# Attention, convolution-gated FFN and spatially gated FFN on one core: a new order of all engines' work

## The chip, the cores and the metric

The kernel runs on one core of a Trainium2 chip. A core has TensorE (PE: matrix multiplications, with its weight loads shown apart as PEld), VectorE (DVE), ScalarE (ACT), GpSimd (POOL) and SyncE (SP), which here only issues DMAs. The metric is the device time of one launch in microseconds (us); lower is better.

## The reference

Three stages follow each other, all in fp32; the output of each is the input `x` of the next.

```python
# attention: q, k, v are (4, 8, 576, 64); block = 64
scores = scale * q @ k.T;  scores = where(block_i >= block_j, scores, -1e9)
attn = exp(scores - max(scores));  attn = attn / (sum(attn) + 1e-9);  out = attn @ v
# first FFN: x is (4, 576, 512), w_in (512, 1024), conv_w (3, 1024), w_out (1024, 512)
h = max(x @ w_in, 0);  conv_out[s] = sum over k of conv_w[k] * h[s + k - 1]
x = (h * sigmoid(conv_out)) @ w_out
# second FFN: w_in (512, 1024), w_spatial (576, 576), w_out (512, 512)
h = max(x @ w_in, 0);  u, v = h[..., :512], h[..., 512:]
v_n = (v - mean(v)) / sqrt(var(v) + 1e-6)
v_s = einsum('ts,bsd->btd', w_spatial, v_n) + b_spatial[:, None]
out = (u * v_s) @ w_out
```

## The kernel before

**Precision.** TensorE reads a 4-byte type with fewer mantissa bits (fp32r) at one pass a column. Each operand is therefore split in a high part, `hi = round(x)`, and a low part, `lo = x - hi`, and a product is three matmuls (hi·hi, lo·hi, hi·lo). In the names of the trace `kp`, `qp` are the high parts of a pair's keys and queries, and the low parts are written over the loaded data in `raw`; `x` holds the two parts of what goes into the first FFN, `w1i_h`, `w1i_l`, `w1o_h`, `w1o_l` those of its weights. A split is two operations (a cast or rounding, then a subtraction), and each can stand on any of ACT, DVE and POOL.

**Steps.** PE's program is a row of 432 steps. The letters of the string `SEQ` say of which kind the next one is:

- `x`: of a pair of heads (there are 16 pairs) four steps that give block scores for a bound on each row's maximum (L943, and L661 for the last block, whose queries stand in `qlast`), and a fifth that transposes the collected maxima `mx` (L1005). DVE reduces the four into `mx` (L948, L983, L986), joins them (L996, task `max_up`), and after the transpose `mt` goes by DMA into a row `mq` (L1018). So x20 to x23 are pair 4's maxima and x24 its transpose.
- `s`: four steps a pair with the masked scores (L1062 in plain fp32 in some pairs, L1070 with split operands in the others; L1074 adds the row `mq`), each followed by an exponential on ACT (L1083). The score buffers `st` are three, shared with the maxima and `v`.
- `v`: attention times values (L669). ACT or DVE then copies the sums into `srow` (L1173) and the product into `xp` (L1164), which frees the buffer. The sums go by two DMAs through a reciprocal (L1188) and come back as `rb`; `xp` times `rb` (L1202) is split into `x`.
- `m`: first FFN (L661): up to 12 matmuls of 288 or 290 columns each. Those that end the FFN are taken out of `mo` by ACT or DVE as `y` (L1276, L1277).
- `p`: second FFN, at the end; `f`: filler.

`x`'s block steps, `s` and `v` use PE's array split in parts of 64 rows or columns (the trace shows 64\*128 or 128\*64), transposes, `m`, `p` and the last block's step the whole array (128\*128). I call these split mode and whole mode.

**Order.** Nothing is left to the hardware or to a compiler's scheduler. `SEQ` fixes PE's order; the tables `ORDER` fix the order of tasks on DVE, ACT, POOL and of DMAs on SP's queue, `ENG` gives for each operation that can be done by several engines the one that does it, and `BIND` which buffer of a ring each step takes. Every engine takes its list strictly in order: an operation that waits holds up what stands behind it. The constants of a planner (`od.cost += ...`) stand beside the matmuls; with all tables given they no longer choose an order.

**Data.** The keys and queries of a pair come in one 576 KB load (L868) into `raw`; there are three such buffers, and in a pair with split operands the loaded data leave theirs when both low parts have been written to another one; pair 5's load waits in this way for pair 3's low parts. Weights of the first FFN come as `w_raw` and `x` halves (L810) and are put together by a copy `top` (L817) and DVE (L820), task `split64`.

Of the kernel before, what the change touches and what calls it, by code (L numbers as in the profile page):

```python
# [1873 lines left out]
```

## Time and profile before

| | us |
|---|---|
| three runs | 578.92, 580.26, 580.30; median 580.26 |
| profiled execution | 579.51 |
| its span, from the first to the last instruction | 577.7 |
| PE busy | 567.5 (98% of the span) |
| DVE, ACT, POOL busy | 420.0, 260.1, 121.3 |

The time of the profiled execution is 1.8 us more than its span; that share lies outside the instructions. A row of the timeline gives start, length, engine, line, operation, output and inputs, sizes, the count of equal operations joined in it, and in brackets the idle time of the engine just before it with what ended that. Matmuls overlap, so for PE the distance from one start to the next is the step of its clock, not the length of one. The granted clock of TensorE is 1.00 over the whole span.

### The profile page before, as it was taken

The page shows a single profiled execution, that of the slowest core. Times are in us where ns is not written, and L with a number is a line of the kernel's source. Part 1 is how long each engine was busy: PE and PEld are TensorE (multiplying, and loading weights), DVE is VectorE, ACT ScalarE, POOL GpSimd, SP SyncE. Part 2 cuts the span into 40 slices and gives each one's busy share as a digit, 9 for nine tenths or more (in the row PEclk, how much of TensorE's full clock was granted, in tenths as well). Part 3 has the DMA queues.
Part 4 walks back from the last instruction along what each step waited for, and adds up shares of the span by engine and source line. Part 5 has one row for each costly group of instructions (what it writes and reads, how often), then busy time and mean ns, then how long its engine had stood idle before and what let it go on. Part 6 is the DMA issues. An engine that isn't in the chain of part 4 may idle for free.

```text
span 577.7 us, 11721 instructions
## 1 busy us (share of the span) xinstructions
PE 567.5 (98%) x4570; PEld 510.3 (88%) x4570; DVE 420.0 (73%) x954; ACT 260.1 (45%) x554; POOL 121.3 (21%) x166
## 2 busy tenths in 40 slices
PE   7999999999999999999999999999999999999997
PEld 5667689798988888899989999999999989999997
DVE  5779889978498889859575788566996445456557
ACT  5657668643566336447353766443351014004101
POOL 3334312130012222400311020333111111012020
PEclk9999999999999999999999999999999999999999
DMA  6666652031404134040214547137303230340002
GB/s 214 222 198 210 211 176 64 31 117 44 125 24 138 55 127 127 15 135 2 65 43 147 194 143 215 43 114 249 101 1 124 71 92 1 124 116 8 32 32 83
DMA packets 43430, 61.13 MB, mean 106 GB/s; under 512 B 8877, under 2 KB 34221, under 8 KB 43374
## 3 DMA queue, kind: packets, MB, share of 16 engines
q1 hardware_dynamic: 43226, 60.37, 32.8%
q8 instruction: 36, 0.59, 0.4%
q14 instruction: 20, 0.16, 0.1%
q10 hardware_dynamic: 148, 0.01, 0.0%
HBM read 45.99 MB, written 14.23 MB: 104 GB/s over the span
## 4 chain that ended last, share of the span: by engine, by line
PE 92%; DMA 2%; ACT 2%; DVE 2%; POOL 1%; issue 1%; SPq 0%; ACTq 0%; DVEq 0%; POOLq 0%
PE mo L661 55%; PE s L661 14%; PE st L669 10%; PE st L1070 4%; PE st L1062 3%; PE st L943 2%; PE st L1074 2%; PE st L661 1%; DMA raw<-in_kq_dram 1%; DMA cwr<-in_cw_dram 1%; ACT e L1083 1%; DVE y L1668 0%; POOL x L698 0%; PE st L1005 0%; ACT top L817 0%
## 5 line engine op out<-in xcount | busy, mean ns | idle before, releaser
L661 PE MATMUL mo<-x,w1i_h 128*128 128x290 f32 x504 | 105.6, 299 | 0.4 <-DVE y L1277 0.4
L661 PE MATMUL mo<-g,w1o_h 128*128 128x288 f32 x464 | 97.7, 297 | 0.0
L661 PEld LDWEIGHTS mo<-x,w1i_h 128*128 128x128 f32 x504 | 82.4, 189 | 2.2 <-DVE y L1277 0.6
L661 PEld LDWEIGHTS mo<-g,w1o_h 128*128 128x128 f32 x464 | 76.0, 189 | 2.0 <-issue 1.6
L1240 DVE SCALAR_TENSOR_TENSOR cc<-h,cwt,cc 128x288 f32<-128x288 f32 x128 | 66.4, 532 | 12.5 <-ACT cc L1237 11.5
L661 PE MATMUL mo<-x,w1i_l 128*128 128x290 f32 x252 | 74.8, 297 | 0.0
L661 PE MATMUL mo<-g,w1o_l 128*128 128x288 f32 x232 | 68.5, 295 | 0.0
L1083 ACT ACTIVATE e<-st 128x1024 f32<-128x1024 f32 (+2 forms) x64 | 53.2, 838 | 21.3 <-PE st L1074 20.4
L661 PE MATMUL mo<-x,w2i_h 128*128 128x288 f32 x256 | 51.8, 295 | 0.0
L948 DVE TENSOR_REDUCE mx<-st 128x2 f32<-128x128 f32 (+2 forms) x64 | 42.5, 684 | 9.6 <-PE st L943 9.2
L661 PEld LDWEIGHTS mo<-x,w1i_l 128*128 128x128 f32 x252 | 47.5, 189 | 0.0
L669 PE MATMUL st<-e,v 128*64 128x448 f32 (+4 forms) x384 | 46.7, 392 | 0.1
L669 PEld LDWEIGHTS st<-e,v 128*64 128x64 f32 x384 | 25.0, 137 | 22.9 <-issue 17.0
L661 PEld LDWEIGHTS mo<-g,w1o_l 128*128 128x128 f32 x232 | 43.6, 188 | 0.0
L672 POOL TENSOR_SCALAR g<-ga 128x288 fp32r<-128x288 f32 x40 | 20.2, 516 | 110.5 <-DVE ga L1588 44.1
L661 PEld LDWEIGHTS mo<-x,w2i_h 128*128 128x128 f32 x256 | 41.2, 188 | 0.4 <-ACT u L1562 0.3
L698 POOL TENSOR_TENSOR g<-cc,g 128x288 fp32r<-128x288 f32 x19 | 18.1, 953 | 105.8 <-ACT g L691 70.3
L661 PE MATMUL s<-w2i_h,x 128*128 128x512 f32 x128 | 39.5, 390 | 0.0
L661 PE MATMUL mo<-ws_h,vnh 128*128 128x288 f32 x135 | 39.4, 296 | 0.0
L661 PE MATMUL mo<-x,w2i_l 128*128 128x288 f32 x128 | 37.7, 295 | 0.0
L1074 PE MATMUL st<-mq,mk 64*128 64x320 f32 (+1 forms) x192 | 36.8, 381 | 0.0
L1237 ACT ACTIVATE cc<-h,cwt 128x288 f32<-128x288 f32 x64 | 33.9, 532 | 5.6 <-DVE g L675 2.8
(200 smaller groups left out, 1327.4 us busy)
## 6 DMA issues: line engine op xcount, KB each, us to landing
x2d<-y SPq DMA_DIRECT2D x32, 288.0 KB
x<-x2d SPq DMA_DIRECT2D x16, 576.0 KB
raw<-in_kq_dram SPq DMA_DIRECT2D x15, 576.0 KB
v<-in_vt_dram SPq DMA_DIRECT2D x16, 320.0 KB
rb<-rd SPq DMA_DIRECT2D x32, 144.0 KB
x<-in_w2i_dram SPq DMA_DIRECT2D x8, 512.0 KB
out_dram<-o SPq DMA_DIRECT2D x28, 144.0 KB
w_raw<-in_w1i_dram SPq DMA_DIRECT2D x4, 512.0 KB
```

What stands on the lines that cost most here:

```text
L661: nc.tensor.matmul(o, w, x, start=start, stop=stop)
L669: nc.tensor.matmul(o[row:row + m], w, x, start=start, stop=stop)
L672: nc.gpsimd.tensor_scalar(o, i, 1.0, 0.0, ALU.mult, ALU.add)
L698: P=("POOL", t_ptt(n), lambda: nc.gpsimd.tensor_tensor(o, a, b, ALU.subtract), 0, prio, True))
L943: nc.tensor.matmul(st[:, e, o:o + n], qp[r, 128 * c:128 * c + 128], kp[r, 0:n], start=True, stop=True)
L948: return ("DVE", t_dve(2 * i.shape[-1] * (i.shape[2] if len(i.shape) == 4 else 1)), lambda: nc.vector.tensor_reduce(o, i, AX.X, ALU.max), ...
L1062: nc.tensor.matmul(out, keys(RAW[p][:, 0, :], r), RAW[p][r, 1, q0:q0 + nq], start=True, stop=False)
L1070: nc.tensor.matmul(st[:, e, o:o + nq], keys(kx, slice(64 * e, 64 * e + 64)), qx[e], start=j == 0, stop=False)
L1074: nc.tensor.matmul(st[:, e, o:o + nq], keys(mk, r), q[r, q0:q0 + nq], start=False, stop=True)
L1083: yield ("ACT", t_act(2 * n), lambda: nc.scalar.activation(ex[:, :, e0:e0 + n], st[:, :, 0:n], ACTF.Exp, scale=0.125), 0, 0)
L1237: yield ("ACT", t_act(HT, False, 1), lambda: nc.scalar.activation(cc, h[:, o:o + HT], ACTF.Copy, scale=cwt[:, c, 1:2]), 0, P_G)
L1240: yield ("DVE", t_dve(HT, ptr=1), lambda: nc.vector.scalar_tensor_tensor(cc, h[:, o + e:o + e + HT], cwt[:, c, j:j + 1], cc, ALU.mult, ALU ...
```

## The change

The diff replaces `SEQ`, the tables `ORDER` of DVE, ACT, POOL and SP, most of `ENG`, and a few rows of `BIND`; and constants of the planner. No line that issues an instruction is changed; all lines behind L62 move by one or two numbers. Both programs have the same 432 steps and the same matmuls on PE. ACT's program has 528 operations for 552, POOL's 189 for 161, DVE's 936 for 940.

```diff
 SEQ = (
-    "xxxyxyxsssfsxxssfxyxxvxssssxyxxvxssssxyxxvxssssxyxxvxssssxyxxvsxsfxssyxxvxsmmmmmxxmmxxxmmmmsssmmssvxmxxxmmssxm"
-    "mmmxMmmmxmmmxxvxsmmmxsssssmmmmmmmxmxxvxssmmmmmxvssssssmmmmxxvxssxmmmmxxmxxvssmmxssmxmxmmxxvsxmsssxmxmxxvsmmxsm"
...
+    "xxxyxyxsssfsxxssfxyxxvxssssxyxxvxssssxyxxvxssssxyxxvxssssxyxxvsxsfxyssmxxvxsmmmmmxxmmxxxmmsssssmmmvxxmxxxmmssm"
+    "mmmxMmxmmmxxvmsxmmmmmxmsssssmmmmxmmxxvxssmmmmvxmssssssmmmmmxxvxssxmmmxxmxxvmssxmssmmmxxmxxvxsmsssxmmmxmxxvsxms"
...
-    "KL": "PDPPPDPPDDDDDDPD",
-    "QL": "PDDDPPPDDDDDPDPD",
+    "KL": "PDPPPPPPDDDDDPDD",
+    "QL": "PDDPPDPDDDDDDDPD",
...
-    "X": "PPDDDPDDPDPPDPPD",
+    "X": "PDDDDDPPPDPDDPPD",
...
-    "TOP": "AAAAAAAAAAAAAAAAAAAAAAAA",
+    "TOP": "AAPPPDAPDPDADAAAPDPAPAAA",
...
-        self.cost = (0.12 if self.tile else 0.2) if tile != self.tile else 0.0
+        self.cost = 0.1 if tile != self.tile else 0.0
...
-            od.cost += max(n / 2400 + 0.0145, 0.107)
+            od.cost += max(n / 2400 + 0.0135, 0.107)
...
+            od.cost += 0.18
```

(`KL`, `QL`: subtraction for the low parts of keys and queries, one letter a pair; `X`: that of `x`; `TOP`: the copy `top`; A, D, P are ACT, DVE, POOL.)

**Behind pair 3's scores, POOL.** `raw<-raw,kp` and `raw<-raw,qp` are the low parts of pair 3's keys and queries, `x_624` or `x_625` is the `x` of pair 0 and `x_768` that of pair 1. Before:

```order
L672 TENSOR_SCALAR qlast_153<-raw 64x64
L698 TENSOR_TENSOR raw<-raw,kp_157 128x576
L698 TENSOR_TENSOR x_624<-xp_132,x_624 128x576
L672 TENSOR_SCALAR qlast_153<-raw 64x64
L672 TENSOR_SCALAR kp_155<-raw 128x576
L698 TENSOR_TENSOR w1i_l<-w_f_140,w1i_h 128x4x128
L698 TENSOR_TENSOR x_768<-xp_133,x_768 128x576
```

And after:

```order
L820 CAST top_144<-x_504 128x512
L673 TENSOR_SCALAR qlast_153<-raw 64x64
L699 TENSOR_TENSOR raw<-raw,kp_157 128x576
L699 TENSOR_TENSOR raw<-raw,qp_158 128x576
L699 TENSOR_TENSOR x_625<-xp_132,x_625 128x576
L673 TENSOR_SCALAR w1o_h<-w_f_139 128x512
L820 CAST top_144<-x_649 128x512
L673 TENSOR_SCALAR qlast_154<-raw 64x64
L673 TENSOR_SCALAR kp_157<-raw 128x576
```

POOL now does both low parts of pair 3, no longer the subtraction of pair 1's `x`, and two copies `top` among them.

**The same stretch, DVE,** from pair 4's last maximum (L948 or L949) to its join (L996 or L997) and some rows behind it. Before:

```order
L986 TENSOR_REDUCE mx<-mxl 128x1
L675 TENSOR_TENSOR w1i_l<-w_f_139,w1i_h 128x4x128
L948 TENSOR_REDUCE mx<-st_113 128x2
L948 TENSOR_REDUCE mxu<-st_113 128x2
L692 CAST qp_156<-raw 128x576
L996 SCALAR_TENSOR_TENSOR mx<-mxu,lim,mx 128x8
L1188 RECIPROCAL rc<-rc 36x32
L1202 TENSOR_TENSOR xp_133<-xp_133,rb 128x160
```

And after:

```order
L949 TENSOR_REDUCE mxu<-st_113 128x2
L693 CAST qp_156<-raw 128x576
L1190 RECIPROCAL rc<-rc 36x32
L693 CAST qlast_153<-raw 64x64
L997 SCALAR_TENSOR_TENSOR mx<-mxu,lim,mx 128x8
L1204 TENSOR_TENSOR xp_133<-xp_133,rb 128x160
```

The join stands behind the reciprocal and behind a cast of pair 5's last queries. Further on, ahead of pair 5's join, DVE has these rows after, of which the first, third and sixth have no counterpart on DVE before:

```order
L693 CAST x_775<-xp_133 128x576
L949 TENSOR_REDUCE mx<-st_112 128x2
L676 TENSOR_TENSOR x_775<-xp_133,x_775 128x576
L984 TENSOR_REDUCE mxl<-mo_110 128x1
L949 TENSOR_REDUCE mxu<-st_112 128x2x2
L693 CAST qp_158<-raw 128x576
L676 TENSOR_TENSOR w1o_l<-w_f_139,w1o_h 128x512
L987 TENSOR_REDUCE mx<-mxl 128x1
```

They are the two operations of pair 1's `x`, and a cast of pair 6's queries.

**Around pair 6's transpose, PE.** Before:

```order
L661 MATMUL mo_111<-full 128x222 x2
L1005 MATMUL st_113<-ident,mx 9x128
L1070 MATMUL st_112<-qp_156,kp_155 128x448 x2
L1070 MATMUL st_112<-qp_156,raw 128x448 x2
L1070 MATMUL st_112<-raw,kp_155 128x448 x2
```

And after:

```order
L662 MATMUL mo_111<-full 128x222 x2
L1006 MATMUL st_113<-ident,mx 9x128
L662 MATMUL mo_111<-kp_157,qlast_154 128x288
L662 MATMUL mo_110<-kp_157,qlast_154 128x288
L1071 MATMUL st_112<-qp_156,kp_155 128x448 x2
```

The step that follows the transpose is now one of whole mode.

**Ahead of the step m33, DVE,** where the sums `y` of the first FFN leave `mo`. Before:

```order
L1202 TENSOR_TENSOR xp_133<-xp_133,rb 128x576
L692 CAST x_1911<-xp_133 128x576
L675 TENSOR_TENSOR x_1911<-xp_133,x_1911 128x576
L692 CAST qlast_153<-raw 64x64
L1277 SCALAR_TENSOR_TENSOR y_137<-mo_110,y_137 128x288
```

And after:

```order
L1204 TENSOR_TENSOR xp_133<-xp_133,rb 128x576
L693 CAST x_1898<-xp_133 128x576
L1279 SCALAR_TENSOR_TENSOR y_137<-mo_110,y_137 128x288
L1156 TENSOR_TENSOR es_131<-e_128,e_130 128x896
L1279 SCALAR_TENSOR_TENSOR y_138<-mo_111,y_138 128x288
```

The cast of `qlast` (pair 11) is gone from DVE there, and on PE the step m31, whose sums the first of these `y` takes, stands ahead of the five score steps s35 to s39 and no longer behind them (second row of `SEQ`).

## Rows read from the trace of the kernel before

**Rows 1.** The page: busy time, share of the span, instructions of each engine.

```profile
PE 567.5 (98%) x4570; PEld 510.3 (88%) x4570; DVE 420.0 (73%) x954; ACT 260.1 (45%) x554; POOL 121.3 (21%) x166
```

**Rows 2.** Waits of PE: line, releaser, us in total, times, longest.

```profile
PE st L1005 <- DMA ident<-in_cst_dram: 2.5, 1, 2.5
...
PE st L943 <- ACT e L1083: 0.9, 3, 0.4
PE st L1070 <- ACT e L1083: 0.6, 1, 0.6
PE mo L661 <- DVE y L1277: 0.4, 1, 0.4
PE st L1062 <- ACT xp L1164: 0.4, 1, 0.4
```

**Rows 3.** Timeline of PE, into split mode and back to whole mode.

```profile
95.52 0.29 PE L661 MATMUL mo<-x,w1i_l 128*128 128x290 f32 x1
95.65 0.29 PE L661 MATMUL mo<-x,w1i_h 128*128 128x290 f32 x1
95.87 0.70 PE L1062 MATMUL st<-raw 64*128 64x256 f32 x4
...
99.01 0.40 PE L661 MATMUL mo<-x,w1i_h 128*128 128x290 f32 x1
99.25 0.29 PE L661 MATMUL mo<-x,w1i_l 128*128 128x290 f32 x1
```

**Rows 4.** Timeline of PE at two transposes.

```profile
39.09 0.28 PE L1005 MATMUL st<-ident,mx 128*9 128x128 f32 x1
39.12 0.51 PE L661 MATMUL mo<-kp,qlast 128*128 128x288 f32 x2
...
144.33 0.27 PE L1005 MATMUL st<-ident,mx 128*9 128x128 f32 x1
144.53 0.38 PE L1070 MATMUL st<-qp,kp 64*128 64x256 f32 x2
```

**Rows 5.** Timeline of SP's queue at the start.

```profile
3.69 0.50 SPq L1429 DMA_DIRECT2D ident<-in_cst_dram  x1
```

**Rows 6.** Timelines of POOL, DVE and SP: pair 3's low parts, pair 5's load.

```profile
39.24 1.42 POOL L698 TENSOR_TENSOR raw<-raw,kp 128x576 fp32r<-128x576 f32 x1 [3.65 <-PE st L1074]
...
40.34 0.93 DVE L675 TENSOR_TENSOR raw<-raw,qp 128x576 fp32r<-128x576 f32 x1
...
41.34 0.33 SPq L868 DMA_DIRECT2D raw<-in_kq_dram  x1
```

**Rows 7.** Timelines of DVE and PE up to pair 4's transpose.

```profile
46.98 0.46 DVE L692 CAST qp<-raw 128x576 fp32r<-128x576 f32 x1 [0.42 <-DMA raw<-in_kq_dram]
47.36 0.83 DVE L996 SCALAR_TENSOR_TENSOR mx<-mxu,lim,mx 128x8 f32<-128x8 f32 x1
48.11 0.34 DVE L1188 RECIPROCAL rc<-rc 36x32 f32<-36x32 f32 x1
...
49.03 0.28 PE L1005 MATMUL st<-ident,mx 128*9 128x128 f32 x1
```

**Rows 8.** Timelines of POOL, DVE and ACT from 54 us on.

```profile
54.03 1.87 POOL L698 TENSOR_TENSOR x<-xp,x 128x576 fp32r<-128x576 f32 x1
...
54.54 1.40 DVE L692 CAST qlast<-raw 64x64 fp32r<-64x64 f32 x1
...
55.93 0.65 ACT L1164 ACTIVATE xp<-st 128x576 f32<-128x576 f32 x1 [0.29 <-POOL x L698]
```

**Rows 9.** Timelines of DVE and PE up to pair 5's transpose.

```profile
57.90 0.21 DVE L996 SCALAR_TENSOR_TENSOR mx<-mxu,lim,mx 128x8 f32<-128x8 f32 x1
...
59.82 0.28 PE L1005 MATMUL st<-ident,mx 128*9 128x128 f32 x1
```

**Rows 10.** Timeline of DVE ahead of m33.

```profile
151.37 0.76 DVE L675 TENSOR_TENSOR x<-xp,x 128x576 fp32r<-128x576 f32 x1
153.58 0.18 DVE L692 CAST qlast<-raw 64x64 fp32r<-64x64 f32 x1 [1.45 <-DMA raw<-in_kq_dram]
```

More of the change, by code (lines that the diff above doesn't have):

```diff
@@ L64 @@
 SEQ = (
-    "xxxyxyxsssfsxxssfxyxxvxssssxyxxvxssssxyxxvxssssxyxxvxssssxyxxvsxsfxssyxxvxsmmmmmxxmmxxxmmmmsssmmssvxmxxxmmssxm"
-    "mmmxMmmmxmmmxxvxsmmmxsssssmmmmmmmxmxxvxssmmmmmxvssssssmmmmxxvxssxmmmmxxmxxvssmmxssmxmxmmxxvsxmsssxmxmxxvsmmxsm"
-    "mssmmmxmmmmmmmmmMmmmmmmsvsssmmmmmvmmmmmmmmmmmmmmmmmmmmMmmmmmmmmmmmppmmmmMmmmpppppppppppppppppppppppppppppppppp"
+    "xxxyxyxsssfsxxssfxyxxvxssssxyxxvxssssxyxxvxssssxyxxvxssssxyxxvsxsfxyssmxxvxsmmmmmxxmmxxxmmsssssmmmvxxmxxxmmssm"
+    "mmmxMmxmmmxxvmsxmmmmmxmsssssmmmmxmmxxvxssmmmmvxmssssssmmmmmxxvxssxmmmxxmxxvmssxmssmmmxxmxxvxsmsssxmmmxmxxvsxms"
+    "mssmmmmmmmmmxmmmMmmmmmmssvmssmmmmvmmmmmmmmmmmmmmmmmmmmMmmmmmmmmmmmppmmmmMmpmmppppppppppppppppppppppppppppppppp"
     "pPppPpPpPPpPppppppPpppppppppppppppppppPPPPPPppPPPppppPppppppppppppppppppPPPPPPppPppppppppPpppPpPpPpPpp"
@@ L241 @@
     ),
+    "mq": (
+        "x4:0 x9:1 x14:2 x19:0 x24:1 x29:2 x34:0 x39:1 x44:2 x49:0 x54:1 x59:2 x64:0 x69:1 x74:2 x79:0"
+    ),
+    "e0": (
+        "s0:0 s6:1 s10:0 s14:1 s18:0 s22:1 s26:0 s30:1 s34:0 s38:1 s42:0 s46:1 s50:0 s54:1 s58:0 s62:1"
+    ),
     "wf": (
         "split64:0 split64.2:1 split64.3:0 split64.4:1 split64.5:0 split64.6:1 split64.7:0 split64.8:1 split64.9:0 "
[3 rows of a table removed]
[3 rows of a table added]
     ),
@@ L251 @@
         "split643.2:0 split643.3:0 split643.4:0 split643.5:0 split643.6:0 split643.7:0 split643.8:0"
-    ),
-    "e0": (
-        "s0:0 s6:1 s10:0 s14:1 s18:0 s22:1 s26:0 s30:1 s34:0 s38:1 s42:0 s46:1 s50:0 s54:1 s58:0 s62:1"
-    ),
-    "mq": (
-        "x4:0 x9:1 x14:2 x19:0 x24:1 x29:2 x34:0 x39:1 x44:2 x49:0 x54:1 x59:2 x64:0 x69:1 x74:2 x79:0"
     ),
@@ L276 @@
     ),
-    "es": (
-        "add_up6:0 add_up7:0 add_up8:0 add_up9:0 add_up10:0 add_up11:0 add_up12:0 add_up13:0 add_up14:0 add_up15:0"
-    ),
     "g": (
@@ L284 @@
         "m104:0 m105:1 m106:2 m107:3 m116:4 m117:5 m118:6 m119:7 m120:8 parts0B110POOL:9 parts0B111POOL:a "
[6 rows of a table removed]
[6 rows of a table added]
         "parts3B210POOL:7 parts3B211POOL:a p120:0 p121:1 parts3T20ACT:3 parts3T30ACT:8 parts3B220POOL:9 parts3T21ACT:2 "
[1 row of a table removed]
[1 row of a table added]
+    ),
+    "es": (
+        "add_up6:0 add_up7:0 add_up8:0 add_up9:0 add_up10:0 add_up11:0 add_up12:0 add_up13:0 add_up14:0 add_up15:0"
     ),
@@ L300 @@
     "cc": (
[4 rows of a table removed]
[4 rows of a table added]
     ),
     "y": (
-        "m14:0 m15:1 m18:0 m19:1 m27:0 m28:1 m31:0 m32:1 m46:0 m47:1 m51:0 m50:1 m59:1 m60:0 m63:0 m64:1 m78:1 m79:0 "
-        "m83:1 m82:0 m91:1 m92:0 m95:1 m96:0 m110:1 m111:0 m114:1 m115:0 m123:0 m124:1 m127:0 m128:1 prep_p2:01"
+        "m14:0 m15:1 m18:0 m19:1 m27:0 m28:1 m31:0 m32:1 m46:0 m47:1 m50:1 m51:0 m59:1 m60:0 m63:0 m64:1 m78:1 m79:0 "
+        "m82:0 m83:1 m91:1 m92:0 m95:1 m96:0 m110:1 m111:0 m114:1 m115:0 m123:0 m124:1 m127:0 m128:1 prep_p2:01"
     ),
@@ L316 @@
     "vf": (
-        "p0:0 p1:1 p2:0 p3:1 p4:0 p21:1 p22:0 p23:1 p24:0 p59:1 p60:0 p61:0 p62:1 p63:0 p94:1 p95:0 p97:1 p96:0"
+        "p0:0 p1:1 p2:0 p3:1 p4:0 p21:1 p22:0 p23:1 p24:0 p59:1 p60:0 p61:0 p63:0 p62:1 p94:1 p95:0 p97:1 p96:0"
     ),
@@ L328 @@
     "o": (
-        "p33.2:0 p34.2:1 p33.2:2 p33.2:3 p34.2:1 p33.2:0 p34.2:2 p34.2:3 p53.2:1 p54.2:2 p53.2:3 p53.2:0 p54.2:1 "
+        "p33.2:0 p34.2:1 p33.2:2 p33.2:3 p33.2:0 p34.2:1 p34.2:2 p34.2:3 p53.2:1 p54.2:2 p53.2:3 p53.2:0 p54.2:1 "
         "p54.2:2 p53.2:3 p54.2:3 p88.2:0 p89.2:2 p88.2:3 p88.2:1 p89.2:0 p88.2:2 p89.2:3 p89.2:1 p124.2:1 p125.2:0 "
@@ L335 @@
 ENG = {
-    "WH": "APDDPDAAPDPPDAAAADAPPDPD",
-    "W": "PDPPPDDPDDDPDPDDPPPDDPDD",
-    "K": "AAPPDPAAADDADAADP",
-    "Q": "DADAPDAAAAPAAPPDA",
-    "QE": "PPPAAADDPDPADPPAADAADPDAPDDPAPAA",
-    "KL": "PDPPPDPPDDDDDDPD",
-    "QL": "PDDDPPPDDDDDPDPD",
-    "M": "AADDDADDAADAAAAD",
-    "ADD": "PPPPPPPPDDDDPPPPDDDDDDDDDDDDDDPDDDDDDDPDDDDDDDPPDDDDDDDPDDDPDDDD",
-    "V": "AAAADAADAAADADAA",
-    "S": "AAAAAAAAAAADDADA",
-    "XH": "AAAPAADDDPAPPDAD",
-    "X": "PPDDDPDDPDPPDPPD",
-    "GH": "ADAAPAAPPAAADADPDAAAADDPPDPAAAAADAADPDADPDDPDAADDAADAADAAADAAPPA",
-    "G": "DPPDDPDDDPPDDPDDDPPPPDDPDDDDDPPDDPDDDDDPPPDDDDDPDDDDDDDDDDDPDDDD",
-    "TOP": "AAAAAAAAAAAAAAAAAAAAAAAA",
+    "WH": "PAPPAAPDPPDPPADPDAPPADDA",
+    "W": "PPDPDPDDDDDDDPDDDPPDDPPP",
+    "K": "AAPDDAPPPAPPDAAAD",
+    "Q": "DPPPDDDAPADPDPADA",
+    "QE": "PAAADAPDPDADPDPADPAPAPAADPDDDDAP",
+    "KL": "PDPPPPPPDDDDDPDD",
+    "QL": "PDDPPDPDDDDDDDPD",
+    "M": "DADDADDAAAAADDAD",
+    "ADD": "PPPPPPPPDDDDPPPPDDDDDDDDDDDPDDDPDPPPDPDDDDDDDDPDDDDPPDDPPDPDDDDD",
+    "V": "AAAAADAAADADDAAA",
+    "S": "AAAAADAAAADDDAAA",
+    "XH": "ADAAAPPDAAAAPDDD",
+    "X": "PDDDDDPPPDPDDPPD",
+    "GH": "AADAAADDDPPAAAPDPPDAAADDPPPPAPAPAAAPADDADPAAAPDDADPAAAAADPAAAAPP",
+    "G": "DDPPPPDDPDPDPPDPDPPDPDPPDPPPDPDDDDDDPPPDDDDDDDDDDDDDDDDDDPDPDPDD",
+    "TOP": "AAPPPDAPDPDADAAAPDPAPAAA",
 }
@@ L667, in tiled @@
             m, n = w.shape[-1], x.shape[-1]
-            od.cost += max(4 * n / 2400, 0.2) / 2 if m == 64 else n / 2400 + 0.022
+            od.cost += max(4 * n / 2400, 0.2) / 2 if m == 64 else n / 2400 + 0.014
             nc.tensor.matmul(o[row:row + m], w, x, start=start, stop=stop)
@@ L816, in split64 @@
         yield alt("TOP", unit,
-                  A=on("A", 512, lambda: nc.scalar.activation(o, x, ACTF.Copy), prio),
+                  A=("ACT", t_act(512, False) + 0.17, lambda: nc.scalar.activation(o, x, ACTF.Copy), 0, prio, False),
                   D=on("D", 512, lambda: nc.vector.tensor_copy(o, x), prio, fast=True),
@@ L943, in fn @@
                     nc.tensor.matmul(st[:, e, o:o + n], qp[r, 128 * c:128 * c + 128], kp[r, 0:n], start=True, stop=True)
-                od.cost += max(n / 2400 + 0.015, 0.105)
+                od.cost += max(n / 2400 + 0.06, 0.16) + (0.055 if i else 0.0)
             def task():
@@ L1005, in fn @@
             nc.tensor.transpose(st[0:NBLK, 0, 0:128], mx[:, 0:NBLK], ident)
-            od.cost += 0.1
+            od.cost += 0.04
             def task():
@@ L1075, in unit @@
             if part is None:
-                od.cost += 5 * nq / 2400 + 0.12 if f32_scores(p) else 4 * max(nq / 2400 + 0.015, 0.105)
+                od.cost += (5 * nq / 2400 + (0.04 if nq > 192 else 0.075) if f32_scores(p) else 4 * max(nq / 2400 + 0.033, 0.076))
             else:
```

239 rows, old and new, of tables (BIND, ORDER) are left out of this document.

## The prediction

> **What bounds the kernel now.** I read the page first: PE is busy for 567.5 of 577.7 us, the next engine, DVE, for 420.0 [rows 1]. The kernel is bound by PE's own row of steps, and since the change keeps every matmul, it can only touch three things: the idle time of PE, the time that PE loses between steps of different kinds, and what the other engines newly make PE wait for. So the second view is the list of what PE waited for [rows 2]. It names one large wait, 2.5 us for the DMA of `ident` ahead of the first transpose, and then a handful of 0.2 to 0.6 us each, of which I copy the largest four kinds, 2.3 us together. Most of these are round trips: PE gives scores, ACT takes the exponential, PE may go on in the freed buffer. The order of PE's steps in that stretch (the first 67 steps, to about 68 us) and the buffers they take are the same after the change, so the three waits of L943 and the one of L1070 for an exponential, 1.5 us, stay. What is there to be won is small, then: the first wait, and two of 0.4 us that are not round trips. What can be lost is not bounded so closely, because between 25 and 100 us DVE is nearly full and runs just ahead of PE.
>
> **Head.** `ident` is the third DMA behind pair 1's load on SP's queue, issued at 3.69 us [rows 5]; after the change it is the first, ahead of a 512 KB weight load. The transpose can then start earlier, by the whole 2.5 us at most. But PE's next steps need more than the transpose: the row `mq` that goes by DMA, ACT's share of the copies around it, and pair 1's 576 KB, which stand behind the same bytes on the queue as before (a 64 KB load that changes places with larger ones ahead of it moves nothing behind it). I take 0.3 us as gained, nearer to the end at which the wait is only moved to the next load; the ends are 0 and −1.6 (the wait falls to the size of one weight load less).
>
> **Pair 3's low parts and pair 5's load.** Before, POOL made the low part of the keys (39.24, 1.42 us) while DVE made that of the queries (40.34, 0.93 us, to 41.27), and SP issued pair 5's load at 41.34, as soon as both were done [rows 6]. After, POOL makes both, one behind the other: 39.24 + 2 × 1.42 = 42.08, so the load starts 0.81 us later. DVE's cast of pair 5's queries at 46.98 waited 0.42 us for that very load [rows 7], so it moves to 47.79 and ends at 48.25. Before, pair 4's join L996 followed at once, and PE's transpose at 49.03 came 0.84 us after the join's end at 48.19. After, the reciprocal (0.34) and a cast of the last queries stand ahead of the join. With an undisturbed cast of 0.18 [rows 10] and join of 0.21 [rows 9] the join ends at 48.25 + 0.34 + 0.18 + 0.21 = 48.98, just in time for 49.03. But while POOL runs, the same two operations took 1.40 and 0.83 [rows 7, 8], and POOL casts pair 5's keys at the same landing; with these the join ends at 50.82, and PE waits 1.8 us. I take 0.4, nearer to the undisturbed end, because only the join's row of this very place is lengthened (by 0.6); ends 0 and 1.8.
>
> A rule of the Trainium skill speaks against this part: "SBUF — State Buffer", section "Who interferes with whom", says that DVE and GpSimd share one pair of ports, held by one of them exclusively, and that the loser is blocked. The rows above agree (1.40 against 0.18 us beside POOL's subtraction of 1.87), and by the rule alone the end at 1.8 would be the one to take; 28 more operations on POOL give it more places.
>
> **Pair 1's `x`.** ACT's copy `xp` at 55.93 stood 0.29 us idle for POOL's subtraction, which ran from 54.03 to 55.90 [rows 8], and PE's L1062 waited 0.4 us for that copy [rows 2]. After, DVE does the cast and the subtraction, in its list well ahead of that point. I count −0.3; the ends are −0.4 and 0 (DVE late too). The price is on DVE: between the joins of pairs 4 and 5 its list has grown by three operations, a cast (0.46, as [rows 7] shows for one of the same size), a subtraction (0.76 [rows 10]) and a cast of pair 6's queries (0.46), 1.68 us together. Pair 5's join ended at 58.11, and the transpose that needs it started at 59.82, 1.71 us later [rows 9]. So the cover is used up to the last 0.03 us. I cost it at nothing, with the next term for what is late beside it.
>
> **The step m33.** On DVE, the sums `y` that free `mo` for m33 stood behind a cast of pair 11's `qlast`, and DVE sat idle 1.45 us until the load had landed [rows 10]; PE lost 0.4 us [rows 2]. After, that cast is gone from DVE, and PE does m31 ahead of s35 to s39, so the sums are ready some microseconds sooner. Ahead of them on DVE stands only the product with `rb`, which needs a DMA of its own; hence 0 as the upper end. I take −0.4, the lower end is −0.55.
>
> **Changes of mode on PE.** The step from 95.65 to 95.87, whole to split mode, took 0.22 against the usual 0.13 (95.52 to 95.65), 0.09 more; on the way back the first matmul took 0.24 (99.01 to 99.25), 0.11 more [rows 3]. Counting along `SEQ`, there are 55 changes before and 63 after, so four pairs more, 4 × 0.20 = 0.80 us. Against it stand three transposes that were followed at once by a step in split mode (pairs 6, 10 and 11): it took 0.20 us to that step (144.33 to 144.53) where a transpose before whole mode takes 0.03 (39.09 to 39.12) [rows 4]. After, all 16 are followed by whole mode, so these three changes cost 0.09 at a later step in place of 0.17: 0.80 − 3 × 0.08 = +0.56. Each price is from one place, and the 0.11 of the way back weighs most; if it is nothing behind the shorter matmuls that end many score steps, 0.44 of this go. I take +0.3, the middle; the ends are 0 and +0.8.
>
> The Trainium skill, "TensorEngine Tiling (Array Packing)", section "Key Properties", says that a change of mode requires the array to drain. Here the rows agree, in the 0.09 and 0.11 above. By the rule alone all eight changes cost, 0.8 us and nothing comes back at the transposes; the sum would be 0.5 higher.
>
> **New waits.** From 70 us to 180 us nearly every step of DVE, ACT and POOL has another place. Where slack was large it is mostly still large, but a wait like that of m33 came up once in 577 us in the order before; I allow +0.3 for one such, ends 0 and +1.2 (a blocked cast as in [rows 8], on the path). The second FFN's steps and the stores at the end stand as they did.
>
> **The sum:** −0.3 + 0.4 − 0.3 − 0.4 + 0.3 + 0.3 = 0.0 us. The profiled execution took 579.51; it lies between the fastest run (578.92) and the median (580.26), 0.75 below the latter. I make the sum against it and forecast 579.5 us, no change. About 1.7 us, 0.3%, is what a measurement can tell from none.
>
> **Rivals.**
>
> *Faster.* The first transpose's wait goes and what it gained is kept to the end: −1.6, with −0.4 for pair 1's `x`, −0.55 for m33, and the other terms at their lower ends, 0: −2.55, 577.0 us. For it speaks that 2.5 us is by far the largest wait, and that PE behind it is limited by nothing but itself for most of the span; against it that pair 1's load and the exponentials' round trips behind it are not moved, and that pair 5's load must not be late. It decides whether pair 4's transpose comes earlier than 49.03.
>
> *Slower.* DVE falls behind pair 5's load. It waits in order for that load ahead of pair 4's join (1.8 us at PE, if POOL disturbs), then carries 1.7 us more work towards pair 5's join with no slack left, of which I count 0.8, and the first steps of the first FFN meet the same late DVE. With the head's 0.3 lost too, and the changes of mode at 0.3 and one new wait at 0.3, less 0.7 for the two waits that go: +1.8 + 0.8 + 0.3 + 0.3 − 0.7 = +2.5, 582.0 us. It decides from the point at which the join of pair 4 ends later than its transpose could start, that is from a delay of the load by more than 0.86 us or one blocked cast. For it speak the two lengthened rows and the thin slack; against it that DVE had idle time of 0.42 at this load and 0.88 a few microseconds on, and that POOL could begin the low parts sooner, having less ahead of it there.
>
> *Nothing moves.* The waits that go come back elsewhere, because most of PE's idle time is round trips of fixed length. That gives 579.5 as well, and I count it with the forecast.
>
> **How the numbers follow.** No change: 0.56. Faster by over 0.3%: 0.21, the first rival with the part of its range that reaches beyond 1.7 us. Slower by over 0.3%: 0.23, the second rival. The range runs from 577.4 to 581.9: below it lies about a third of the first rival's chance, above it somewhat over half of the second's, 2 in 10 together.
>
> **What would show it.** In the profile of the changed kernel: PE's wait for `ident` well below 2.5 us, but pair 4's transpose still within 0.5 us of 49.0; SP's issue of pair 5's load at about 42.2 and DVE's cast behind it ending near 48.3; no wait of PE's L1062 for `xp` beyond 0.2 and none of L661 for `y`; and PE's busy time within 0.5 us of 567.5. I would be wrong if PE's transposes of pairs 4 to 6 wait for `mx` by over 1 us, if the first FFN's steps show waits for `x`, `g` or `y` that together exceed 1 us, or if pair 4's transpose starts before 48.

## The result and the profile after

The changed kernel takes 583.62 us (median of four runs, 582.98 to 583.77), the kernel before on the same chip 579.59: a ratio of 1.0072, 95% interval 1.0055 to 1.0088. On a second chip it was 581.70 against 578.87, 1.0043 (1.0027 to 1.0058). It is slower, by 0.4 to 0.7%, where no change was forecast; the range ended at 581.9. The profiled execution took 583.57, with a span of 581.8 us against 577.7.

The page's first part, in the columns of [rows 1], then PE's waits in those of [rows 2]:

```profile
PE 567.5 (98%) x4570; PEld 510.3 (88%) x4570; DVE 425.5 (73%) x950; ACT 245.7 (42%) x530; POOL 143.1 (25%) x194
```

```profile
PE st L1006 <- DVE mx L997: 3.0, 1, 3.0
PE st L944 <- DVE mxu L949: 1.3, 1, 1.3
...
PE mo L662 <- DVE y L1279: 1.0, 1, 1.0
PE st L1063 <- DVE mxu L949: 1.0, 1, 1.0
PE st L944 <- DVE mt L1012: 0.9, 1, 0.9
PE st L1071 <- ACT e L1084: 0.6, 1, 0.6
PE st L944 <- ACT e L1084: 0.5, 2, 0.3
```

PE is busy for exactly as long as before. All of the loss is idle time, and four waits of about 1 us each that [rows 2] does not have stand for it; all four name DVE. The wait for `ident` is gone from the list, but the first transpose waits no less: the name in front is now the join L997, which was nearly as late before.

Since both programs have the same steps, the starts of the same steps can be set side by side (read from PE's timelines of both kernels):

| step | before | after | later by |
|---|---|---|---|
| first transpose (x4) | 10.26 | 9.88 | −0.38 |
| pair 0, second half of the scores (s4) | 15.84 | 15.64 | −0.20 |
| next score step (s5) | 17.14 | 18.09 | 0.95 |
| pair 2, fourth block step (x13) | 24.37 | 26.73 | 2.36 |
| pair 4, second block step (x21) | 39.56 | 42.08 | 2.52 |
| pair 4, third block step (x22) | 39.90 | 43.52 | 3.62 |
| pair 4's transpose (x24) | 49.03 | 52.63 | 3.60 |
| pair 4's second score step, behind `xp` (s19) | 56.64 | 59.80 | 3.16 |
| pair 6's transpose (x34) | 68.57 | 72.05 | 3.48 |
| m28 | 141.16 | 144.34 | 3.18 |
| m33 | 154.18 | 156.81 | 2.63 |
| m116 | 348.34 | 351.13 | 2.79 |
| m117 | 349.95 | 353.93 | 3.98 |
| last step of the program | 573.21 | 577.14 | 3.93 |

The loss comes in four jumps, at s5 (1.15), x13 (1.41 up to it), x22 (1.10) and m117 (1.19), 4.85 together. Between them 0.7 us net is won, at s19 (0.44) and m33 (0.55) above all. Three of the jumps lie ahead of 45 us, in the stretch in which PE's own order is unchanged.

What DVE did there, in its timeline after:

```profile
16.60 1.24 DVE L781 TENSOR_SCALAR cwr<-cwr 128x24 uint32<-128x24 uint32 x1
17.76 0.28 DVE L949 TENSOR_REDUCE mxu<-st 128x2 f32<-128x128 f32 x1
...
23.88 2.59 DVE L676 TENSOR_TENSOR w1i_l<-w_f,w1i_h 128x512 fp32r<-128x512 f32 x1 [0.86 <-POOL w1i_h L673]
26.40 0.61 DVE L949 TENSOR_REDUCE mxu<-st 128x2 f32<-128x128 f32 x2
...
41.71 1.57 DVE L1204 TENSOR_TENSOR xp<-xp,rb 128x160 f32<-128x160 f32 x1 [0.77 <-DMA rb<-rd]
43.20 0.27 DVE L1012 CAST mt<-st 9x128 fp32r<-9x128 f32 x1
```

And POOL's at the same times:

```profile
16.55 1.26 POOL L699 TENSOR_TENSOR w1i_l<-w_f,w1i_h 128x512 fp32r<-128x512 f32 x1
...
23.81 0.24 POOL L673 TENSOR_SCALAR qlast<-raw 64x64 fp32r<-64x64 f32 x1
24.01 1.28 POOL L699 TENSOR_TENSOR w1i_l<-w_f,w1i_h 128x512 fp32r<-128x512 f32 x1
25.27 0.67 POOL L673 TENSOR_SCALAR qp<-raw 128x576 fp32r<-128x576 f32 x1
...
41.69 1.41 POOL L699 TENSOR_TENSOR raw<-raw,kp 128x576 fp32r<-128x576 f32 x1 [0.63 <-PE st L1075]
```

PE's timeline shows who stood behind each of them:

```profile
18.09 0.54 PE L1063 MATMUL st<-raw 64*128 64x320 f32 x2 [1.02 <-DVE mxu L949]
...
26.73 0.50 PE L944 MATMUL st<-kp,qp 64*128 64x512 f32 x2 [1.32 <-DVE mxu L949]
...
43.52 0.44 PE L944 MATMUL st<-kp,qp 64*128 64x384 f32 x2 [0.94 <-DVE mt L1012]
...
353.93 0.40 PE L662 MATMUL mo<-x,w1i_h 128*128 128x290 f32 x1 [1.03 <-DVE y L1279]
```

Three times the pattern is the same. An operation that PE does not need soon (a bit operation on the convolution weights, the low part of a weight, a product of pair 1) stands in DVE's list ahead of one that PE needs at once (a reduction, the copy `mt`), and POOL works at that moment. The first takes 1.24 us for 24 elements a partition, the second 2.59 us; the same subtraction takes 0.68 where POOL is quiet (below). POOL was first each time, ahead of the second by 0.07 us with a short cast (23.81). At m117 it is another matter: ACT takes m115's sums only at 352.98, and one of the two buffers `y` was still being stored, by a DMA that stood behind a 512 KB load on SP's queue:

```profile
345.78 0.33 SPq L811 DMA_DIRECT2D x<-in_w2i_dram  x1
347.01 0.38 SPq L1282 DMA_DIRECT2D x2d<-y  x1
```

### The profile page after: what moved, and what is told of

It reads as the page before. It is cut to its first block, busy times and chain, and to the rows that moved or that the text cites. A ratio compares the mean times of both kernels' runs of the same rounds, so it can differ in the third digit from the quotient of the medians.

```text
span 581.8 us, 11708 instructions
## 1 busy us (share of the span) xinstructions
PE 567.5 (98%) x4570; PEld 510.3 (88%) x4570; DVE 425.5 (73%) x950; ACT 245.7 (42%) x530; POOL 143.1 (25%) x194
## 4 chain that ended last, share of the span: by engine, by line
PE 94%; DVE 2%; ACT 1%; DMA 1%; issue 1%; SPq 0%; POOL 0%; ACTq 0%; DVEq 0%
PE mo L662 56%; PE s L662 14%; PE st L670 10%; PE st L1071 4%; PE st L1063 3%; PE st L944 2%; PE st L1075 2%; PE st L662 1%; DMA raw<-in_kq_dram 1%; ACT e L1084 1%; DVE w1i_l L676 0%; PE st L1006 0%; DVE mx L949 0%; DVE w_f L821 0%; SPq L860 0%
## 5 line engine op out<-in xcount | busy, mean ns | idle before, releaser
L949 DVE TENSOR_REDUCE mx<-st 128x2 f32<-128x640 f32 (+2 forms) x64 | 42.6, 683 | 5.9 <-PE st L944 5.5
L1246 DVE SCALAR_TENSOR_TENSOR cc<-cc,h 128x288 f32<-128x288 f32 x64 | 29.2, 466 | 10.2 <-ACT cc L1244 10.0
```

The source lines that it names most:

```text
L949: return ("DVE", t_dve(2 * i.shape[-1] * (i.shape[2] if len(i.shape) == 4 else 1)), lambda: nc.vector.tensor_reduce(o, i, AX.X, ALU.max), ...
L1246: yield ("DVE", t_dve(HT), lambda: nc.vector.scalar_tensor_tensor(cc, cc, 1.0, h[:, o:o + HT], ALU.add, ALU.mult), 0, P_G, True)
```

## The experiments

**Theory.** Each of the four jumps is one operation in the wrong place of a list, and the length of DVE's operations there is POOL's doing: moved, each gives its time back. **Rivals.** PE is held by round trips there anyway and the wait comes back (the prediction's "nothing moves"); only DVE's order counts, POOL has no part in it.

**One move at a time.** The first moves the bit operation (task `start2`) behind pair 1's join:

```diff
-x7 ends2 x5 start2 x7 x8*2 max_up1 start2 split64.3
+x7 ends2 x5 x7 x8*2 max_up1 start2*2 split64.3
```

> After the change, with one DVE task moved: the bit operation on the convolution weights (L781, 1.24 us at 16.60, beside a subtraction on POOL from 16.55 to 17.81) stands behind pair 1's join instead of ahead of its last reductions. PE's fourth score step of pair 0 waited 1.02 us for a reduction behind it. Theory 'DVE's list': the time that a DVE operation takes beside POOL, and what is queued behind it, holds PE; then this wait falls below 0.2 us, pair 1's transpose starts near 18.7 instead of 19.61, and the time falls by 0.9 to 1.1 us. Rival 'round trips': PE is held there by the exponentials on ACT in any case, the wait comes back at the next steps, and the shift of all later work stays within 0.3 us of what it was. Rival 'clock': the loss is the granted clock of 0.50 between 9 and 15 us, and the place of this operation changes nothing.

580.97 us against 578.77 of the kernel before on that chip, 1.0039 (1.0021 to 1.0058). The bit operation takes 0.17 us (at 18.07), the wait at s5 is gone, and pair 1's transpose starts at 18.20, by 1.4 us sooner than in the changed kernel. The jump at x13 went with it, without being touched:

```profile
18.07 0.17 DVE L781 TENSOR_SCALAR cwr<-cwr 128x24 uint32<-128x24 uint32 x1
...
22.42 0.69 DVE L676 TENSOR_TENSOR w1i_l<-w_f,w1i_h 128x512 fp32r<-128x512 f32 x1 [0.85 <-POOL w1i_h L673]
...
22.64 0.56 POOL L673 TENSOR_SCALAR qlast<-raw 64x64 fp32r<-64x64 f32 x1 [0.26 <-DMA raw<-in_kq_dram]
...
38.83 1.38 DVE L693 CAST qlast<-raw 64x64 fp32r<-64x64 f32 x1
```

DVE now started the subtraction at 22.42, ahead of POOL's short cast, which had to wait for its load (22.64), and it took 0.69. This time it was POOL's operation that was lengthened, to 0.56 from 0.24. So up to x19 this execution is 0.14 us ahead of the kernel before. Then a cast of `qlast` fell beside POOL's subtraction (from 38.76) and took 1.38 instead of 0.18, and PE waited 1.15 us for it and 0.67 for the copy behind it. The theory's cause is confirmed, its forecast of the gain is not: in the profiled execution, the slowest of eight (579.76 to 583.41), the gain was lost to the same cause at the next place.

The second move puts the weight's subtraction behind a large reduction:

```diff
-split64.4 x11 split64.3 x12 x11 x10*2 x13 split64.5
+split64.4 x11 x12 x11 x10*2 x13 split64.3 split64.5
```

> After the change, with one DVE task moved: the subtraction for a weight's low part (2.59 us at 23.88, 0.68 where POOL is quiet; 0.86 us of waiting for POOL ahead of it) stands behind the large reduction of pair 2's third block step and no longer ahead of the reductions that PE's step at 26.73 waited for (1.32 us). Theory 'DVE's list': that wait goes but for 0.2, the time falls by 1.1 to 1.4 us. Rival 'round trips': the next score steps wait for ACT instead, and at most 0.4 us is won. If only the order counts and POOL has no part in the length of 2.59, the subtraction keeps that length at its new place with POOL idle; if POOL has, it falls to about 0.7.

581.04 us, 1.0040 (1.0025 to 1.0055). From pair 1's transpose to x13 it is 5.73 us, against 7.12 in the changed kernel and 5.72 in the one before. In its timeline the subtraction, with POOL idle since 26.51, has its usual length:

```profile
26.76 0.68 DVE L676 TENSOR_TENSOR w1i_l<-w_f,w1i_h 128x512 fp32r<-128x512 f32 x1
```

The third puts the copy of the maxima ahead of the product with `rb`:

```diff
-max_up3 ends4 norm_a0 x19 x20 norm_a0
+max_up3 ends4 x19 norm_a0 x20 norm_a0
```

> After the change, with one DVE task moved: the copy of pair 3's transposed maxima (43.20) stands ahead of the product with the returned sums, which waited 0.77 us for its DMA and took 1.57 us beside POOL's subtraction. Theory 'DVE's list': the copy starts within 0.1 us of the transpose's end, at about 41.7, PE's wait of 0.94 us at 43.52 goes, and the time falls by 0.9 to 1.1 us. Rival: the maxima's next step then waits for something else (the reductions behind the product, now 0.3 later), and at most 0.4 is won.

582.32 us, 1.0060 (1.0044 to 1.0076). The wait at x22 is gone; from x21 to x22 it is 0.34 us as before the change, for 1.44. This execution shows something else besides. Its first 40 us are ordered as in the changed kernel, and yet the wait at s5 is missing. DVE's timeline, then POOL's:

```profile
15.84 0.16 DVE L781 TENSOR_SCALAR cwr<-cwr 128x24 uint32<-128x24 uint32 x1
```

```profile
15.89 1.27 POOL L699 TENSOR_TENSOR w1i_l<-w_f,w1i_h 128x512 fp32r<-128x512 f32 x1
```

DVE was first by 0.05 us, and took 0.16 where it takes 1.24 when POOL is first by 0.05 (16.55 and 16.60 above). One microsecond of PE's time hangs on which of two engines starts first.

The fourth is on SP's queue: the store of m111's sums goes ahead of the load.

```diff
-m110 split643.5 m111 load_tails
+m110 m111 split643.5 load_tails
```

> After the change, with one DMA moved on SP's queue: the store of m111's sums (issued at 347.01) stands ahead of the 512 KB weight load (345.78). The sums of m115 take the same buffer, and ACT began them at 352.98, 1.85 us after the step had ended. Theory 'store behind a load': the store lands sooner, ACT takes the sums near 351.2, PE's wait of 1.03 us at m117 goes, and the time falls by 1.0 to 1.2 us. Rival: the store's landing hangs on the loads of transposed data issued behind it (347.44), or on DVE's late sums at 346.5; then the wait stays above 0.7.

581.98 us, 1.0057 (1.0041 to 1.0073). ACT took the sums at 350.52, waiting for nothing but the step itself, and m117 followed m116 after 1.60 us, where it is 2.80 in the changed kernel. The wait is gone as expected.

How firm each of the four waits is can be counted over the profiled executions in which its own move was not made, counting in the later ones of the swaps on POOL and of the changed kernel. The wait at m117 is there in all six (0.96 to 1.57 us). The one at s5 is there in four of five with POOL's list as it was (0.92 to 1.02), and the one at x13 in four of five (1.32 each time). The one at x22 is there in two of six only (0.94 and 0.67). In the other four `rb` came sooner, and the product of pair 1 ended ahead of POOL's subtraction (in the second trace of the changed kernel it started at 40.60 and took 0.33). So the run with the third move alone does not show that its move took this wait away.

**POOL's part.** DVE's list stays as it is, and POOL changes the places of two pairs of neighbours:

```diff
-one201 one200 split64.2 split64.3 ... split64.4 one301 split64.5 split64.6
+one201 one200 split64.3 split64.2 ... split64.4 split64.5 one301 split64.6
```

> After the change with DVE's list untouched; on POOL two pairs of neighbours change places: a copy (0.76 us) goes ahead of the subtraction that ran beside DVE's bit operation, and a copy goes ahead of the cast of pair 3's queries that ran beside DVE's subtraction. Theory 'POOL holds DVE up': the bit operation, 1.24 us, takes at most 0.9, and the subtraction, 2.59 us, at most 2.0; PE's waits at 18 and 26.7 us fall by 0.3 to 0.7 each. Rival 'only the order on DVE': both keep their lengths, and PE its waits.

582.11 us on the second chip, 1.0052 (1.0034 to 1.0069), with the changed kernel at 581.70 beside it. Here it is the timelines that decide, DVE's first:

```profile
15.97 0.16 DVE L781 TENSOR_SCALAR cwr<-cwr 128x24 uint32<-128x24 uint32 x1
...
22.79 1.97 DVE L676 TENSOR_TENSOR w1i_l<-w_f,w1i_h 128x512 fp32r<-128x512 f32 x1 [0.85 <-POOL w1i_h L673]
```

```profile
22.72 0.24 POOL L673 TENSOR_SCALAR qlast<-raw 64x64 fp32r<-64x64 f32 x1
22.92 1.28 POOL L699 TENSOR_TENSOR w1i_l<-w_f,w1i_h 128x512 fp32r<-128x512 f32 x1
```

POOL was waiting for a load when DVE came to the bit operation, which took 0.16, and the wait at s5 went. In its place another operation of DVE (L821, at 17.83) met POOL's subtraction and took 1.74 for 0.68, but no wait of PE followed from it. The subtraction on DVE lasted until 24.76, which is 0.56 us after the last of POOL's two operations in a row, the short cast and the subtraction, had ended (24.20). In the changed kernel it lasted until 26.47, 0.53 after the last of three (25.94), and PE's wait at x13 fell from 1.32 to 0.82. So DVE did not slow down, it stood still until POOL had no operation in a row, and then took about its own time. POOL's part is shown, with DVE's order untouched. The profiled execution, the shortest of four, took 581.29, by 2.28 us less than the changed kernel's; the wait at x22, which the swaps do not touch, is missing here too and is part of that. The medians show no gain: the runs (581.29 to 583.16) overlap with the changed kernel's.

**All four moves, and more.**

> After the change with all four moves at once (the bit operation behind the join, the weight's subtraction behind the reduction, the copy of the maxima ahead of the product, the store ahead of the load). Each of them took its wait away in a run of its own; the single runs moved all later work by 0.5 to 1.5 us. Theory 'DVE's list': the waits are independent and add up, the time falls by 3.5 to 4.5 us against the changed kernel, to the time of the kernel before or up to 1 us below it. Rival 'the wait moves on': in the run with the first move alone, PE lost what it had gained at pair 3's and pair 4's steps; if that is the rule, all four together give no more than 2 us.

579.49 us against 578.87 of the kernel before and 581.70 of the changed kernel on that chip: 1.0012 of before (0.9996 to 1.0027). Of the four waits of DVE none is left in PE's list:

```profile
PE st L1006 <- DVE mx L997: 2.7, 1, 2.7
PE mo L1385 <- DVE eps L1399: 1.2, 1, 1.2
PE st L1071 <- ACT e L1084: 0.6, 1, 0.6
PE st L944 <- ACT e L1084: 0.5, 2, 0.3
PE mo L662 <- ACT h L1236: 0.3, 1, 0.3
PE st L1063 <- DVE mxu L949: 0.2, 1, 0.2
```

The last step starts at 573.07, 0.14 us sooner than in the first trace of the kernel before and 4.07 sooner than in that of the change. The medians say less, 2.2 us, for the changed kernel's runs there reach from 581.33 to 583.57 and hit different waits. The gain that the theory gave, 3.5 to 4.5 us, is that of the traces and not that of the medians. That the four moves together undo the change's loss is shown, up to the 0.3% that the interval leaves open; that they bring it below the kernel before is not.

They do so without DVE meeting POOL less often. In the whole traces I count the operations of DVE that took over 0.3 us more than the shortest of the same operation, data and size in any run: 19 in the kernel before, 30 in the changed kernel, 31 with all four moves. In every trace each of them ran beside an operation of POOL. None is a reduction: 75 to 84 reductions a trace ran beside POOL, and none took over 0.08 us more than its shortest. What the moves change is who stands behind the lengthened operations.

Two variants go on from there: pair 3's low part of the queries back on DVE (`QL`, fourth letter), and then also, on ACT, m118's result ahead of two operations that wait for DVE.

```diff
-m114 m115 m116*2 m117 m116 m117 m116 m118 m117 m118 m117
+m114 m115 m116*2 m117 m118 m116 m117 m116 m117 m118 m117
```

> All four moves, and pair 3's low part of the queries back on DVE, where the kernel before has it, so that DVE and POOL work on the two halves side by side. By the prediction's own term the load of pair 5 is issued 0.8 us sooner than with both on POOL, which is worth 0 to 1.8 us at pair 4's transpose, 0.4 as taken there. If that term is right, 0.3 to 0.5 us faster than with the four moves alone; if pair 5's load isn't what pair 4's transpose waits for, the same within 0.2 us, or slower by DVE's 0.9 us of additional work.

> All four moves, the low part of pair 3's queries on DVE, and on ACT the step that takes m118's result out of its buffer (354.20 in the trace of the four moves) ahead of two operations that wait for DVE. In the trace before it, PE waited 0.33 us for it at m120 (0.11 with the low part on DVE). Theory 'lists': that wait goes, 0.2 to 0.5 us less than with the low part on DVE alone, which puts it at the kernel before or up to 0.7 us below it. Rival: the two operations that now stand behind are late in their turn and m121 or the first step of the second FFN waits instead; then nothing is won.

579.73 us, 1.0012 (1.0001 to 1.0022), and 580.33 against 579.14, 1.0011 (1.0000 to 1.0023). The low part on DVE brings pair 5's load 0.32 us sooner (41.66 for 41.98), not 0.8; no difference can be measured. The last variant removes the wait at m120, and the second FFN starts at 355.40 for 356.06; 0.27 us of that was there already at m116, ahead of the move. By step p10 nothing of this is left (390.50 for 390.39). In between, PE's starts at m123 (behind POOL's `g`) and m126 (behind DVE's `y`) come 0.54 us late together, two waits that the run with the low part on DVE alone does not have. The rival came true, at other steps than it named: the wait moved on.

**The two kernels once more.**

> The changed kernel once more, on the same chip as the others and for one more trace. If the waits named in its first trace (for DVE's reductions at 18.1 and 26.7 us, for the copy at 43.5, for the sums at 353.9) belong to the order, all four are there again with lengths within 0.3 us; if they hang on the timing of a single execution, one or two of them are missing, and the time varies by over 1 us from run to run.

581.70 us (581.33 to 583.57). Its profiled execution, the longest of the five, has the waits at s5 and x13 again, 0.98 and 1.32 us long. That at m117 is longer, 1.57 for 1.03, and here ACT's row names the store that it waited for:

```profile
353.12 0.41 ACT L1278 ACTIVATE y<-mo 128x288 fp32r<-128x288 f32 x1 [3.31 <-DMA x2d<-y]
```

That at x22 is missing, and a wait of 0.74 for a reduction on DVE at pair 5's step x28 is new. So two of the four waits come in the same place with the same length, and the others change with the execution.

> The kernel before once more, for a second trace of it. If its waits belong to its order, all of those in the first trace of 0.3 us and more are there again (for the identity matrix's load, for the exponentials at 50.3, 61.0 and 67.4, for pair 1's copy at 56.6, for the sums at 154.2), each within 0.2 us, and no operation of DVE takes over 1.5 us. If single executions decide, some are missing and others are new.

578.82 us (578.00 to 579.47). Its profiled execution took 578.00, by 1.5 us less than the first one. The round trips at 50.0, 60.6 and 67.1 are there with the same lengths, and so is the wait at s19. The one at m33 is missing:

```profile
152.54 0.19 DVE L692 CAST qlast<-raw 64x64 fp32r<-64x64 f32 x1 [0.80 <-DMA raw<-in_kq_dram]
152.65 0.44 DVE L1277 SCALAR_TENSOR_TENSOR y<-mo,y 128x288 fp32r<-128x288 f32 x1
```

Pair 11's load landed 5.3 us after its issue (147.13) instead of 6.05, and DVE's sums were in time. A third of what separates the two executions (0.55 of 1.5 us) is this wait; so a gain counted from one trace can be a gain over that execution alone. Against the expectation, two single operations of DVE take over 1.5 us (1.59 at 187.43, 1.76 at 373.31), as they do in the first trace. So in the kernel before DVE is held up by POOL too, but PE has no wait there.

**The two gains alone,** in the kernel before: POOL's subtraction of pair 1's `x` goes ahead of a weight's, and the cast of `qlast` behind the sums.

```diff
-norm_a7*3 ends11 m31 add_up8 m32 m34*2
+norm_a7*3 m31 add_up8 m32 ends11 m34*2
...
-one500 split64.8 norm_a1 split64.9
+one500 norm_a1 split64.8 split64.9
```

> The kernel before, with only the two gains that the prediction counted on: on POOL the subtraction of pair 1's x goes ahead of a weight's subtraction (52.79), so that ACT's copy at 55.93 no longer waits for it, and on DVE the cast of pair 11's qlast goes behind the two sums ahead of m33. The prediction's terms: 0.3 us for the first, in every execution; 0.4 for the second, 0 in executions in which pair 11's load lands sooner, as it did in the second trace of the kernel before. Together 0.3 to 0.8 us faster than before. Rival: what follows (the exponentials' round trips at 61.0 and 67.4, the sums after m33) takes them back; then the same within 0.1 us.

578.60 us against 579.00, 0.9994 (0.9981 to 1.0008): no change that can be measured. ACT's copy no longer waits, and from x27 to s19 PE needs 5.92 us for 6.33. By pair 5's first score step (s22) 0.17 of the 0.41 is left, the rest went into the round trips between them. At m33 there is no wait, as in the second trace of the kernel before.

## Why the prediction was wrong

**The bound.** Right: PE busy 567.5 in both, and everything is decided by what PE waits for. The conclusion that failed stands right there. Because PE's first 67 steps and their buffers are the same, the waits were said to stay. Three of the four named did (0.22, 0.27 and 0.57 us). But no new ones were looked for in that stretch: the work of the other engines in the first 40 us was not set side by side, except at the places where a term had been found. The lists of DVE, POOL and SP are new there. Three of the four jumps are in this stretch, 3.66 of 4.85 us.

**Head.** Right in size: −0.38 at the transpose, −0.20 left at s4, for −0.3 taken. Why it is no more can be seen in the profile after: behind `ident` (landed at 10.12 before) the join was next, ended at 9.94 before and 9.83 after. The list of waits names only the last releaser; the next one was 0.2 us behind.

**Pair 5's load.** The term cost nothing. In the changed kernel the transposes of pair 4 waited for nothing, the delay at x22 having given DVE time. With the four moves, where PE is as early as before, it can be read without that. DVE's timeline, then PE's:

```profile
47.72 0.45 DVE L693 CAST qp<-raw 128x576 fp32r<-128x576 f32 x1
48.16 0.34 DVE L1190 RECIPROCAL rc<-rc 36x32 f32<-36x32 f32 x1
48.54 0.19 DVE L693 CAST qlast<-raw 64x64 fp32r<-64x64 f32 x1
48.76 0.23 DVE L997 SCALAR_TENSOR_TENSOR mx<-mxu,lim,mx 128x8 f32<-128x8 f32 x1
```

```profile
49.17 0.28 PE L1006 MATMUL st<-ident,mx 128*9 128x128 f32 x1
```

The join ends at 48.99, which is the undisturbed end of the term (48.98), and PE starts 0.18 later. The load itself was issued 0.64 us later than before (41.98 for 41.34), of the 0.81 forecast. The disturbed end, 50.82, did not come. The row that the 0.4 leant on (0.83 us for the join) was as real as the others of its kind, only not at this place any more.

**Pair 1's `x`.** −0.44 at s19 for −0.3 taken, but 0.32 comes back by pair 6's transpose, the round trips being what they are. The 1.68 us of additional work on DVE cost nothing: pair 5's transpose did not wait.

**m33.** −0.55 against the trace before, as the term's lower end has it. The second trace of the kernel before has no such wait, so against the kernel, not against that execution, it is worth between 0 and 0.55.

**Changes of mode.** Between x34 and m116 the shift falls by 0.69, of which 0.55 is m33. All else in that stretch, the eight changes and the three transposes among it, comes to −0.14, where +0.3 was taken and 0 the lower end. The Trainium skill's rule on draining ("TensorEngine Tiling (Array Packing)", "Key Properties"), which alone would give +0.8, does not come out as a net cost here; the sum of all is what the runs show, the single prices were not measured again.

**New waits.** This is the term that failed: +0.3 with an upper end of 1.2 for one wait of m33's kind, where there were four jumps of 1.1 to 1.4, 4.85 together. It looked for them from 70 to 180 us, where the order of the steps changes; the four lie at 18, 27, 44 and 354 us, and between 72 and 350 us the changed kernel has no wait in PE's list. The one at m117 is a store behind a load, for which no term stood. For the other three the rows for the price were there. A cast blocked for 1.2 us and a join for 0.6 [rows 7, 8] show that beside POOL an operation can take several times its length. From that a price per meeting follows, and the change puts 28 more operations on POOL. How often they meet DVE ahead of something that PE needs was not looked up, and was set at less than one. The number of meetings alone would not have told it, as the count under the four moves shows.

**The rival *slower*** has the right sign and the right mechanism (DVE held up by POOL, PE waiting behind it in order) at 582.0, but put it behind pair 5's load; that its number comes nearest of the three is luck. Its place was the head, and its second part, DVE's fuller list at pair 5's join, did not occur. The Trainium skill's "SBUF — State Buffer", "Who interferes with whom", was cited as speaking against the change, for one place. It says that the loser is blocked for the whole instruction and that the order of issue decides; the runs agree on both, with 0.16 us when DVE was first by 0.05 and 1.24 when POOL was. They show one thing more, that the loser also waits through POOL's next operations when these follow at once.

**What should have shown it.** Of the signs named ahead, PE's busy time came true, and so did the vanished wait for `xp`. Pair 4's transpose, which was to stay within 0.5 us of 49.0, came at 52.63, and pair 5's load was issued at 44.75 for 42.2, both late from the jumps ahead of them. The wait for `y` is gone at m33, but has come back at m117. The sign for being wrong, a sum of over 1 us in waits for `y` in the first FFN, was met by m117 alone.

**Open.** Why the median of the POOL swaps does not follow its trace; why `rb` came late in the first trace of the changed kernel; why m123 and m126 waited in the last variant; and which of the waits each unprofiled run met. That the spread of the changed kernel's runs (over 2 us on the second chip) is the toss between DVE and POOL is argued from three traces, not shown.

## What to carry to other kernels

When an engine's list changes, set its rows side by side for the whole program, also where the engine that bounds the kernel keeps its order, and look in each list for an operation that nobody needs soon standing ahead of one that somebody needs now. Where two engines can block each other, price an operation by its blocked length (here up to 8 times the usual) wherever the other is at work, look up what stands behind it at each such place, and move work off the blocked engine's critical spots before moving it between engines. A wait read from one execution may not be there in the next, and behind its releaser often stands another, a tenth of a microsecond earlier.

## What the runs showed of the hardware

A short idle time of PE can cost more than itself. In the run with the first move alone, PE waited 1.15 and 0.67 us near 41 us. This table by stretches gives the stretch, its length, the busy time of PE, PEld, DVE, ACT and POOL (instructions), the granted clock, the DMA share and GB/s:

```profile
40.00:41.00 1.00, 0.64 (x6) 0.50 (x6) 0.97 (x2) 0.00 (x0) 1.00 (x2) 1.00 0.92 262
41.00:42.00 1.00, 0.33 (x6) 0.13 (x4) 1.00 (x3) 0.00 (x0) 0.53 (x1) 0.79 0.97 349
42.00:43.00 1.00, 1.00 (x6) 0.67 (x8) 1.00 (x4) 0.00 (x0) 0.00 (x0) 0.50 0.61 241
43.00:44.00 1.00, 1.00 (x8) 0.49 (x6) 1.00 (x4) 0.57 (x1) 0.00 (x0) 0.50 0.08 21
44.00:45.00 1.00, 1.00 (x6) 0.28 (x4) 1.00 (x3) 0.12 (x1) 0.81 (x1) 0.51 0.90 194
45.00:46.00 1.00, 1.00 (x8) 0.42 (x6) 1.00 (x3) 0.00 (x0) 0.60 (x1) 1.00 0.84 336
```

The clock fell to the lower of its two levels, 1.2 GHz, for some 3 us, and the 24 matmuls of the `v` step, 2.92 us in the other traces, took this time:

```profile
42.58 4.09 PE L670 MATMUL st<-e,v 128*64 128x128 f32 x24
```

That is 1.17 us on top of 1.82 us of waiting. In the changed kernel's own trace the granted clock is 0.50 from about 8.8 to 15.6 us, behind the wait for the first join. That does not explain its loss: with all four moves it is 1.00 throughout, with the swaps on POOL 0.50 in the same stretch, and from the first transpose to x7 (9.94 to 13.73, and 9.97 to 13.76) both take the same time. In the kernel before with the two gains alone it is 0.50 there as well, and that execution took 578.22.
